# First units loaded as pairs of chunks, W1 in quarters, one PSUM pool and a new order, in a fused RWKV and squared-ReLU kernel

## The chip, the cores and the metric

The kernel runs on one core of a Trainium2 chip. The metric is the device time of one execution in microseconds (us). Three executions took 174.83, 175.56 and 176.46 us, median 175.56. A further execution was profiled; its span, from the first to the last instruction, is 173.7 us.

The core has a matrix engine (PE, with its weight loads shown as PEld), a vector engine (DVE), a scalar engine (ACT), GpSimd (POOL) and a queue engine for transfers (SP). ACT and POOL can issue transfers too. All transfers run on the same 16 DMA engines. Each engine works through its own instructions in order.

## The reference

Two parts follow each other. An attention with a decaying state, over 4 batches, 8 heads, 768 tokens and a head size of 48:

```python
for t in range(S):
    cur = einsum('bhd,bhe->bhde', u * k[t], v[t])
    y[t] = einsum('bhd,bhde->bhe', r[t], state + cur)
    state = w * state + einsum('bhd,bhe->bhde', k[t], v[t])
x = y.transpose(0, 2, 1, 3).reshape(3072, 384)
h = maximum(x @ w_in, 0)          # w_in 384 x 2048
out = (h * h) @ w_out             # w_out 2048 x 384
```

Inputs and output are float32; the products are made in bfloat16.

## The kernel before, in words

The tokens of a batch are cut into 6 chunks of 128, which gives 24 units of one batch and one chunk each. For a unit, r, k and v are tiles of 128 tokens by 8 heads by 48. Inside a chunk the recurrence becomes products: k is scaled by a power of w that falls with the token (`kh`, with the table `Wk`), r by the inverse power (`rh`, with `Wt`), both into the bfloat16 tile `rk`. They are transposed, either on PE (`T`, followed by a copy `Tc` out of PSUM) or by a DMA transpose (`XB`), into `rkT`. `A` makes the 128 by 128 products of k and r for each head, into two banks; `Bm` multiplies them by a triangular mask. `Y` adds the masked products times v (`vb`, v in bfloat16) and, from the second chunk of a batch on, r times the state `S0W`. `U` makes the product of k and v that goes into the state, `S0` (first chunk) or `ts` and `S` (later ones) update it. The term with u is made on the side: `P0` is r times k, `P1` times u, `du` the sum over a head, `dv` that sum times v; `xs` adds it to Y. `X` transposes xs on PE and `xTc` copies it out, or `xX` transposes by DMA.

The FFN takes units in groups: the first two groups have one unit, the other eleven have two. `F1` is a slice of x @ w_in into one PSUM bank (12 products of 128 columns for a single unit, 6 of 256 for a pair; four slices for a single unit, eight for a pair), `re` the ReLU into bfloat16, `sq` the square. `F2` adds a quarter of the second product into one bank for each unit, in the order 0, 1, 2, 3; `os` copies it to SBUF, `out` stores it.

Nothing is scheduled at run time. The string `ORDER` (lines 21 to 106) lists all steps; the loop at lines 499 to 511 takes them one after the other, and each step goes to the engine that stands behind its colon (A, D, G for POOL, P, S for SP). The numbers after the slashes are buffers. So the order of the string, restricted to an engine, is the order of that engine's queue. A step whose input is not ready, or whose buffer is still in use, holds its engine.

What the change touches:
- Units are numbered chunk by chunk: units 0 to 3 are the first chunks of the four batches (`i % B` is the batch, `i // B` the chunk). Each of r, k and v of a unit is one transfer of 128 tokens by 8 heads, in rows of 48 floats, 192 bytes (`ld`, line 319).
- W1 (w_in) comes in slices of 256 columns: seven by `lW` (line 323) into one of four float32 buffers, cast by `cW` (line 259 or 261), one by a casting transfer that POOL issues (`W`, line 332). W2 (w_out) comes in four casting transfers from POOL.
- w goes by DMA to 4 partitions (line 273) and is spread by a shuffle on DVE (line 282); u likewise.
- PSUM has eight banks in three pools: four for the attention, two for F1 (`bH`), two for F2 (`bO`). The early tables `Wk` and `Wt` lie in the two banks of F2 until it starts.
- `Z` (line 480) multiplies the identity into a bank that is not read; the order of before has 139 blocks of 128 columns of it in the first 20 us.

Of the kernel before, what the change touches and what calls it, by code (L numbers as in the profile page):

```python
# [8 lines left out]
FP32 = mybir.dt.float32  # L9
BF16 = mybir.dt.bfloat16  # L10
# [5 lines left out]

GROUPS = [1, 1, 2, 2, 2, 2, 2, 2, 2, 2, 2, 2, 2]
EARLY = 4
POOLS = dict(ldr=7, ldk=7, ldv=7, ws=0, wsa=4, rk=7, P0=5, dv=5, vb=8, rkT=7, bank=4, bankH=2, bankO=2, Bm=6, xs=5, xT1=2, xT2=3, xT4=1, hr=6, hq=30, os=4, ts=2)
ORDER = """  # L20
ld.r.1:S/0 w:A ld.k.1:S/0 u:S Z.48.5:P tab:A ld.k.0:S/1 ld.k.2:S/2 shw:D ld.r.0:S/1 logw:A ld.r.2:S/2 Wt:A/0 P0.1:D/0
shu:D Wk:A/1 lW.0.6:S/0 rh.1:D/0 kh.1:D ld.v.1:S/0 ld.k.3:S/3 T.1:P/0 kh.0:D/1 Z.16.5:P P1.1:G Tc.1:A/0 kh.2:D/2 rh.0:D
ld.v.3:S/1 WtS:A rh.2:D P0.2:G/1 A.1:P/1/2 WkS:A T.0:P/3 lW.0.1:S/1 Z.16.5:P P1.2:D ld.r.3:S/3 Tc.0:A/1 du.1:D/0
P0.0:D/2 cW.0.6:A ld.v.0:S/2 A.0:P/0/3 dv.1:G Bm.1.1:D/0 Z.6.5:P du.2:D/1 T.2:P/2 P1.0:G Bm.1.0:D/1 ld.v.2:S/3 Z.22.5:P
Tc.2:A/2 Bm.0.0:D/2 Bm.0.1:D/3 lW.0.0:S/2 vb.1:A/0 lW.0.5:S/3 kh.3:D/3 Y.1:P/1 cW.0.1:A lW.0.7:S/0 A.2:P/0/2 xs.1:D/0
Z.4.5:P P0.3:G/3 vb.3:A/1 du.0:D/2 lW.0.4:S/1 X.1:P/3 Z.8.5:P rh.3:D wc:S xTc.1:A/0 Bm.2.0:D/4 vb.0:A/2 T.3:P/1
ld.k.4:S/4 dv.0:D Y.0:P/3 Z.13.5:P Tc.3:A/3 vb.2:G/3 Bm.2.1:D/5 P1.3:G xs.0:D/1 A.3:P/0/2 X.0:P/1 cW.0.0:A U.0:P/3
dv.2:G Bm.3.0:D/1 Z.6.7:P xTc.0:A/1 du.3:D/3 lW.0.3:S/2 F1.1.0:P/0 Bm.3.1:D/0 ld.r.4:S/4 F1.0.0:P/1 re.1.0:D/0 W.1.0:G
W.0.2:G cW.0.7:G Y.2:P/0 Y.3:P/1 re.0.0:A/1 ld.k.5:S/5 xs.2:D/2 cW.0.5:A dv.3:D F1.1.3:P/0 cW.0.4:A X.2:P/2 F1.0.3:P/1
re.1.3:D/2 ld.r.5:S/5 xTc.2:A/0 W.1.1:G U.2:P/0 xs.3:D/3 F1.0.2:P/0 re.0.3:A/3 sq.1.3:D2/0 WLcol:A X.3:P/2 F1.1.2:P/1  # L30
re.0.2:D/4 xTc.3:A WLm:G U.3:P/1 F1.2.1:P/0 re.1.2:A/5 W.1.2:G sq.0.3:A0/1 F1.2.5:P/1 re.2.1:D/2 W.1.3:G sq.0.0:A0/2
U.1:P/2 S0.2:D re.2.5:A/3 F1.2.4:P/0 sq.0.2:D2/3 cW.0.3:A S0.0:D F1.2.7:P/1 re.2.4:D/1 sq.1.0:A0/4 F2.0.0:P/1
sq.2.5:D2/5 re.2.7:A/4 S0.3:D F1.0.1:P/0 F1.2.3:P/1 re.0.1:D/0 F2.1.0:P/0 S0.1:D re.2.3:A/3 F1.1.1:P/0 sq.1.2:D2/6
sq.0.1:D2/7 ld.k.7:S/6 F1.2.0:P/1 re.1.1:A/5 F2.0.1:P re.2.0:A/0 sq.1.1:D2/8 F1.2.2:P/0 sq.2.4:A0/9 sq.2.0:D1/10
F2.1.1:P kh.4:D/4 F1.2.6:P/1 ld.v.5:S/4 rh.4:D P0.4:D/4 F2.1.2:P ld.r.7:S/6 re.2.2:D/5 P1.4:G F2.0.2:P re.2.6:D/1
sq.2.2:A0/11 F2.1.3:P ld.v.4:S/5 kh.5:G/5 sq.2.1:A0/12 sq.2.6:D1/13 F2.0.3:P os.1:A/0 du.4:D/4 ld.k.6:S/0 T.4:P/0
sq.2.3:A0/14 rh.5:D F2.2.0:P/0 os.0:A/1 P0.5:D/0 Tc.4:A/4 ld.r.6:S/0 T.5:P/3 P1.5:D F2.2.1:P kh.7:D/6 Tc.5:A/5
ld.v.7:S/6 A.4:P/1/2 du.5:D/0 F2.3.0:P/1 Bm.4.0:D/3 ld.k.9:S/2 A.5:P/0/3 vb.4:A/4 dv.4:G Bm.4.1:D/2 F2.3.1:P vb.5:A/5
ld.r.9:S/2 Bm.5.1:D/4 dv.5:G sq.2.7:A0/15 Y.4:P/1 Bm.5.0:D/5 F2.3.2:P rh.7:G ld.k.8:S/1 xs.4:D/4 U.4:P/2 Y.5:P/3
# [503 lines left out]
```

## Time and profile before

| | us |
|---|---|
| median of three executions | 175.56 |
| lowest, highest | 174.83, 176.46 |
| span of the profiled execution | 173.7 |
| first F1 product starts | 20.48 |
| last product ends | 170.1 |

The page gives, for each engine, the time in which it was busy; `x` counts instructions. A line of a group names the source line, the engine, the operation, the tiles (output, arrow, input), the count, then the busy time, the mean of one instruction in ns, and how long the engine stood idle before them. The groups that matter here:

```profile
L444 PE MATMUL bank<-xT,W 128*128 128x256 bf16 (+1 forms) x624 | 74.5, 264 | 1.3 <-ACT W L259 1.2
L471 PE MATMUL bank<-W,hq 128*128 128x384 bf16 x384 | 73.6, 326 | 0.0
...
L383 DVE TENSOR_TENSOR Bm<-bank,maskJT 128x512 bf16<-128x512 f32 x48 | 31.4, 683 | 3.0 <-PE bank L375 3.0
L345 POOL TENSOR_TENSOR P<-P,ub 128x384 f32<-128x384 f32 x14 | 15.5, 1110 | 30.0 <-DVE P L341 26.8
```

L444 is F1 and L471 is F2. Products overlap in PE's pipeline, so the mean of one is longer than the distance from one to the next; the distances are read from the chain of waits and the timeline. The transfers:

```profile
ldr<-in_r_dram SPq DMA_DIRECT2D x24, 192.0 KB, 3.9
...
wsa<-in_moe_w_in_dram SPq DMA_DIRECT2D x7, 384.0 KB, 5.6
W<-in_moe_w_out_dram POOLq DMA_DIRECT2D x4, 384.0 KB, 7.9
rkT<-rk SPq DMA_TRANSPOSE x14, 3.4
```

The last number is the median time from issue to landing, in us.

### The profile page before, as it was taken

How to read it: one execution, taken by the hardware profiler on the slowest of the kernel's cores; microseconds unless marked ns; L12 is line 12 of the kernel's file. 1: busy time of each engine (PE TensorE's matmuls, PEld its weight loads, DVE VectorE, ACT ScalarE, POOL GpSimd, SP SyncE). 2: the span in 40 equal slices, each digit the busy share in tenths (PEclk: the TensorE clock that was granted, in tenths of full speed). 3: DMA queues.
4: the chain of work that ended last, by engine and by line, in shares of the span. 5: the costliest groups of instructions: out<-in, count | busy, mean ns of one | idle time of the engine just before them, and what ended most of it. 6: DMA issues, size and time to landing. Idle time of an engine off the chain costs nothing.

```text
span 173.7 us, 4402 instructions
## 1 busy us (share of the span) xinstructions
PE 165.4 (95%) x1714; PEld 121.9 (70%) x1714; DVE 140.7 (81%) x278; ACT 109.8 (63%) x203; POOL 69.3 (40%) x84
## 2 busy tenths in 40 slices
PE   4989699999999999999999999999999999999991
PEld 1445498766878787877777787778678677787760
DVE  5989787799899989999989898899998667853520
ACT  2489389557599979786676769659478141173401
POOL 4264743044385694923464950601950301000000
PEclk9999999999999999999999999999999999999999
DMA  5999999999999999989698799989931422110041
GB/s 106 245 249 248 258 213 219 201 192 189 213 188 214 243 171 234 197 191 205 128 217 178 151 205 212 152 191 180 200 94 30 151 94 68 25 45 4 0 171 55
DMA packets 102276, 28.34 MB, mean 163 GB/s; under 512 B 94824, under 2 KB 102256, under 8 KB 102256
## 3 DMA queue, kind: packets, MB, share of 16 engines
q1 hardware_dynamic: 100360, 26.10, 71.4%
q0 software_dynamic: 1744, 1.77, 6.2%
q8 instruction: 13, 0.21, 0.5%
q10 hardware_dynamic: 152, 0.20, 0.3%
q14 instruction: 7, 0.06, 0.1%
HBM read 20.46 MB, written 4.72 MB: 145 GB/s over the span
## 4 chain that ended last, share of the span: by engine, by line
PE 80%; DMA 8%; SPq 6%; ACT 1%; issue 1%; POOL 1%; POOLq 0%
PE bank L471 36%; PE bank L444 33%; DMA wsa<-in_moe_w_in_dram 8%; SPq L319 5%; PE bank L375 3%; PE bank L393 2%; PE bank L391 2%; PE bank L402 2%; PE bank L362 2%; SPq L323 1%; PE bank L428 1%; ACT W L259 1%; ACT hr L452 0%; ACT hq L459 0%; ACT os L259 0%
## 5 line engine op out<-in xcount | busy, mean ns | idle before, releaser
L444 PE MATMUL bank<-xT,W 128*128 128x256 bf16 (+1 forms) x624 | 74.5, 264 | 1.3 <-ACT W L259 1.2
L471 PE MATMUL bank<-W,hq 128*128 128x384 bf16 x384 | 73.6, 326 | 0.0
L452 ACT ACTIVATE hr<-bank 128x512 bf16<-128x512 f32 x71 | 42.0, 597 | 35.9 <-PE bank L444 33.2
L444 PEld LDWEIGHTS <-W 128*128 128x128 bf16 x624 | 55.4, 98 | 11.9 <-ACT W L259 1.4
L471 PEld LDWEIGHTS <-hq 128*128 128x128 bf16 x384 | 35.6, 98 | 17.8
L459 ACT ACTIVATE hq<-hr 128x512 bf16<-128x512 bf16 x57 | 34.7, 629 | 2.5 <-DVE hr L454 2.4
L383 DVE TENSOR_TENSOR Bm<-bank,maskJT 128x512 bf16<-128x512 f32 x48 | 31.4, 683 | 3.0 <-PE bank L375 3.0
L345 POOL TENSOR_TENSOR P<-P,ub 128x384 f32<-128x384 f32 x14 | 15.5, 1110 | 30.0 <-DVE P L341 26.8
L353 POOL TENSOR_TENSOR dv<-ldv,du 128x384 f32<-128x384 f32 x19 | 16.4, 874 | 25.7 <-DVE du L348 21.0
L454 DVE TENSOR_SCALAR hr<-bank 128x512 bf16<-128x512 f32 x25 | 17.1, 689 | 10.4 <-PE bank L444 6.5
L463 DVE TENSOR_TENSOR hq<-hr 128x512 bf16<-128x512 bf16 x35 | 15.0, 457 | 1.9 <-ACT hr L452 1.9
L410 DVE TENSOR_TENSOR xs<-bank,dv 128x384 bf16<-128x384 f32 x24 | 13.2, 553 | 3.5 <-PE bank L393 2.8
L259 ACT COPY os<-bank 128x384 f32<-128x384 f32 x18 | 8.6, 477 | 8.8 <-PE bank L471 8.1
L480 PE MATMUL bank<-identity 128*128 128x512 bf16 (+1 forms) x40 | 11.6, 427 | 2.3 <-POOL identity masks.py:199 2.3
L348 DVE TENSOR_REDUCE du<-P 128x8 f32<-128x384 f32 x24 | 12.9, 543 | 0.0
L341 POOL TENSOR_TENSOR P<-ldr,ldk 128x384 f32<-128x384 f32 x11 | 11.3, 1026 | 3.9 <-DMA ldr<-in_r_dram 3.9
L259 ACT COPY rkT<-bank 128x1024 bf16<-128x1024 bf16 x10 | 10.1, 1015 | 2.9 <-PE bank L362 2.2
L423 POOL TENSOR_TENSOR S0W<-ts,WLm 128x384 bf16<-128x384 f32 x7 | 7.4, 1061 | 10.0 <-PE bank L471 6.7
L393 PE MATMUL bank<-vb,Bm 128*128 128x48 bf16 x192 | 10.8, 183 | 0.3 <-ACT vb L259 0.3
L393 PEld LDWEIGHTS <-Bm 128*128 128x128 bf16 x192 | 9.5, 96 | 1.3 <-issue 0.4
L259 ACT CAST vb<-ldv 128x384 bf16<-128x384 f32 x19 | 9.6, 511 | 0.2 <-DMA ldv<-in_v_dram 0.2
L259 ACT COPY xT<-bank 128x384 bf16<-128x384 bf16 x14 | 6.5, 477 | 5.0 <-PE bank L428 5.0
(61 smaller groups left out, 161.7 us busy)
## 6 DMA issues: line engine op xcount, KB each, us to landing
ldr<-in_r_dram SPq DMA_DIRECT2D x24, 192.0 KB, 3.9
ldk<-in_k_dram SPq DMA_DIRECT2D x24, 192.0 KB, 3.8
ldv<-in_v_dram SPq DMA_DIRECT2D x24, 192.0 KB, 4.0
out_dram<-os SPq DMA_DIRECT2D x23, 192.0 KB, 2.2
wsa<-in_moe_w_in_dram SPq DMA_DIRECT2D x7, 384.0 KB, 5.6
W<-in_moe_w_out_dram POOLq DMA_DIRECT2D x4, 384.0 KB, 7.9
rkT<-rk SPq DMA_TRANSPOSE x14, 3.4
W<-in_moe_w_in_dram POOLq DMA_DIRECT2D x1, 192.0 KB, 8.2
```

The costliest lines, as they stand in the source:

```text
L259: e.copy(o, a)
L345: e.tensor_mul(t, t, ub)
L353: e.tensor_mul(dvb[slot[f"dv{i}"]], loaded("v", i), t)
L383: e.tensor_mul(Bmb[slot[f"Bm{i}{h}"]], heads(bank(f"bA{i}{h}"), 128), mask_b)
L393: e.matmul(y[:, hc, D * h : D * (h + 1)], m[h][:, hc, :], vb[:, 2 * hc + h, :], start=(c == 0), stop=True, skip_group_check=True,)
L410: e.tensor_add(xsb[slot[f"xs{i}"]].rearrange("p (a b) -> p a b", a=HP), heads(bank(f"bY{i}"), 2 * D), dvb[slot[f"dv{i}"]].rearrange("p (a ...
L444: e.matmul(hp[:, fi, :], W1[f // 2][:, c, 128 * (f % 2) : 128 * (f % 2 + 1)], xt[:, c, :], start=(c == 0), stop=(c == CCH - 1), skip_group ...
L452: e.activation(hr, hp, AF.Relu)
L454: e.tensor_scalar_max(hr, hp, 0.0)
L459: e.activation(hq, hr, AF.Square)
L463: e.tensor_mul(hq, hr, hr)
L471: e.matmul(bank(f"bO{i}", "bO")[:, 0:d_model], hqb[slot[f"hq{g},{f // m}"]][:, at : at + L], W2[q][:, f % 4, :], start=(f == 0), stop=(f = ...
```

## The change

Units are listed in a table. Units 0 and 1 are the first two chunks of batch 0, units 2 and 3 those of batch 1; batches 2 and 3 follow, and from unit 8 on the order is chunk by chunk. The first four units are loaded in pairs: partition p of a pair holds tokens 2p and 2p + 1 of the 256, so that a row is 96 floats, 384 bytes, and chunk c of the pair lies in partitions 64c to 64c + 63. A tile that `loaded` gives for such a unit holds the even or the odd tokens of both chunks. `Ap`, `Bp`, and the new branches of `Y` and `U` therefore work on halves of 64 rows, with masks `maskP`; `Y` adds the u term by two products with the identity, so `xs` of these units is a plain copy. For them the transposes of k and r are separate steps (`TK`, `TR`, copies `KC`, `RC`), and the tables have three columns (even, odd, and the plain one for later units).

W1 comes in four transfers of 512 columns into three buffers, cast in halves by ACT, DVE or POOL; none comes by a casting transfer. w goes to all 128 partitions by one transfer, and the shuffle goes. The eight PSUM banks are one pool. The four quarters of F2 may come in any order. The order is new throughout. Counted in the two strings: loads 72 become 60 and 6 of pairs; `XB` 14 become 18, `T` 10 become 2 (and 2 `TK`, 2 `TR`), `X` 14 become 8, `xX` 10 become 16; on POOL `kh` 5 become 15, `rh` 6 become 13, `P0` 11 become 16, `vb` 3 become 11, `cW` 1 become 4; on ACT `re` 71 become 64, `sq` 57 become 44; on DVE `re` 25 become 32, `sq` 39 become 52; fill 139 blocks of columns become 81.

```diff
+UNITS = [(0, 0), (0, 1), (1, 0), (1, 1), (2, 0), (3, 0), (2, 1), (3, 1), (0, 2), (1, 2), (2, 2), (3, 2), (0, 3), (1,
+    3), (2, 3), (3, 3), (0, 4), (1, 4), (2, 4), (3, 4), (0, 5), (1, 5), (2, 5), (3, 5)]
+PAIRED = 4
-POOLS = dict(ldr=7, ldk=7, ldv=7, ws=0, wsa=4, rk=7, P0=5, dv=5, vb=8, rkT=7, bank=4, bankH=2, bankO=2, Bm=6, xs=5, xT1=2, xT2=3, xT4=1, hr=6, hq=30, os=4, ts=2)
+POOLS = dict(ldr=8, ldk=8, ldv=8, ws=3, rk=7, P=5, dv=5, vb=8, rkT=7, bank=8, Bm=8, xs=5, xT1=2, xT2=3, hr=6, hq=28,
+    os=4, ts=2)
 ORDER = """
-ld.r.1:S/0 w:A ld.k.1:S/0 u:S Z.48.5:P tab:A ld.k.0:S/1 ld.k.2:S/2 shw:D ld.r.0:S/1 logw:A ld.r.2:S/2 Wt:A/0 P0.1:D/0
...
+w:A lp.k.0:S/0 tab:A u:S lp.r.0:S/0 lp.r.1:S/1 lp.k.1:S/1 lp.v.0:S/0 logw:A Wk.1:A kh.1:D/0 shu:D Wk.0:A lp.v.1:S/1
+Wt.0:A rh.0:D/1 kh.0:G/1 Wt.1:A rh.1:G/0 P0.0:D/0 wc.1:A lW.1:S/0 P0.1:D/1 Z.56:P/0 TK.0:P/0 KC.0:A/0 rh.2:D/2 Wt.2:A
+P1.0:G lW.0:S/1 P1.1:D du.1:D/0 Z.5:P/1 TR.0:P/1 RC.0:A/1 lW.2:S/2 kh.3:G/3 kh.2:D/2 ld.k.4:S/4 Z.20:P/2 Ap.0.0:P/2/3
+rh.3:D/3 du.0:D/1 vb.0:A/0 wc.0:A P0.3:G/2 TK.1:P/4 ld.r.4:S/4 Ap.0.1:P/5/6 Bp.0.0.1:D/0 dv.1:G TR.1:P/7 vb.2:A/1
+ld.v.4:S/4 vb.3:D/2 dv.0:G Bp.0.1.0:D/1 vb.1:A/3 WLcol:A P1.3:G U.2:P/0 U.1:P/1 Bp.0.1.1:D/2 KC.1:A/2 U.0:P/3 U.3:P/5
+WLm:G RC.1:A/3 Bp.0.0.0:D/3 Y.0:P/6 xs.0:A/0 S0.0:D ts.1:D/0 cW.2:G Y.1:P/4 cW.3:G du.3:D/2 Wk.2:A S0.2:D X.0:P/7
+P0.2:G/3 Ap.1.1:P/2/6 xTc.0:A/0 xs.1:D/1 Ap.1.0:P/3/1 Bp.1.1.0:D/4 cW.1:A W.0:G X.1:P/0 F1.0.1:P/7 P1.2:D xTc.1:A/1
+F1.1.1:P/4 W.1:G cW.0:A lW.3:S/0 ts.3:D/1 re.0.1:A/0 Bp.1.1.1:D/5 F1.0.0:P/0 ld.r.5:S/5 du.2:D/3 cW.4:A cW.5:G dv.2:D
+F1.1.0:P/5 Bp.1.0.0:D/6 re.0.0:A/1 dv.3:G F1.1.2:P/7 Bp.1.0.1:D/7 re.1.0:A/2 ld.k.5:S/5 F1.0.2:P/0 kh.4:G/4 re.1.2:D/3
+sq.1.0:A/0 Y.2:P/5 xs.2:A/2 re.1.1:D/4 rh.4:G/4 re.0.2:D/5 sq.0.2:D/1 Y.3:P/7 P0.4:G/4 T.4:P/5 xs.3:A/3 X.2:P/4
+X.3:P/0 xTc.2:A/0 F2.1.0:P/7 ld.r.6:S/6 xTc.3:D/0 vb.4:G/4 Tc.4:A/4 sq.1.2:D/2 P1.4:G F1.2.4:P/4 F1.2.2:P/0 re.2.4:D/2
...
         def w(e):
-            e.dma_start(out=quarter_rows(wrow), in_=row4(w))
+            e.dma_start(out=wb.rearrange("p a b -> p (a b)"), in_=spread(w, 128))
...
+        def lp(e, x, q):
+            b, c = UNITS[2 * q]
+            e.dma_start(
+                out=ld[x][slot[f"p{x}{q}"]].rearrange("p (h m) -> p h m", h=H),
+                in_=src[x].rearrange("b h (c p a) d -> b c p h (a d)", p=128, a=2)[b, c // 2],
+            )
+
+        def lW(e, q):
+            e.dma_start(out=wsb[slot[f"ws{q}"]], in_=w_in_t[:, :, 512 * q : 512 * (q + 1)])
...
+        def Ap(e, q, a):
+            kT, rT = (
+                rkTb[slot[f"{n}{q}"]].rearrange("p x y -> p (x y)").rearrange("p (h c t) -> p h c t", h=HP, c=2)
+                for n in ("kT", "rT")
+            )
+            for hc in range(HP):
+                for c in range(2):
+                    for h in range(2):
+                        p0 = 64 * h
+                        e.matmul(
+                            heads(bank(f"bA{q}{a}{h}"), 128)[64 * c : 64 * c + 64, hc, :],
+                            kT[p0 : p0 + D, hc, c, 64 * a : 64 * a + 64],
+                            rT[p0 : p0 + D, hc, c, :],
+                            start=True, stop=True, skip_group_check=True,
+                        )
...
         def Y(e, i):
...
+            if i < PAIRED:
+                q, s = i // 2, i % 2
+                rows = slice(64 * s, 64 * s + 64)
+                for a in range(2):
+                    e.matmul(
+                        y[64 * a : 64 * a + 64], identity[rows, rows],
+                        dv_of(2 * q + a)[rows].rearrange("p (a e) d -> p a (e d)", e=2),
+                        start=True, stop=False, skip_group_check=True,
+                    )
...
+                for hc in range(HP):
+                    for h in range(2):
+                        for a in range(2):
+                            e.matmul(
+                                y[:, hc, D * h : D * (h + 1)],
+                                Bmb[slot[f"Bm{q}{a}{h}"]][rows, hc, :],
+                                vbb[slot[f"vb{2 * q + a}"]][rows, 2 * hc + h, :],
+                                start=False, stop=True, skip_group_check=True,
+                            )
+                return
...
         def F2(e, i, q):
...
-                    start=(f == 0), stop=(f == FCH - 1), skip_group_check=True,
+                    start=(seen[i] == 1 and f % 4 == 0), stop=(seen[i] == 4 and f % 4 == 3), skip_group_check=True,
```

## The prediction

> **What bounds the kernel now.** First the page: busy time and the forty slices.
>
> ```profile
> PE 165.4 (95%) x1714; PEld 121.9 (70%) x1714; DVE 140.7 (81%) x278; ACT 109.8 (63%) x203; POOL 69.3 (40%) x84
> ...
> PE   4989699999999999999999999999999999999991
> ...
> DMA  5999999999999999989698799989931422110041
> ```
>
> From the fifth slice on PE has no gap; DVE is near 95% in the middle and the DMA engines are full up to slice 28 of 40. So the time is: when dense work on PE begins, plus the PE work left, plus a tail. The chain of waits says what sets the beginning and the end:
>
> ```profile
> 13.93 5.59 DMA wsa<-in_moe_w_in_dram
> 19.54 0.88 ACT W L259
> ...
> 20.45 8.05 DMA wsa<-in_moe_w_in_dram
> ...
> 163.57 6.51 PE bank L471 x40
> 170.11 0.48 ACT os L259
> ```
>
> The slices of W1 arrive late: one lands at 13.93 + 5.59 = 19.52, ACT casts it, and then the first product of the FFN runs (timeline, both rows PE):
>
> ```profile
> 2.35 5.30 PE L480 MATMUL bank<-identity 128*128 128x512 bf16 x12 [2.35 <-POOL identity masks.py:199]
> ...
> 20.48 1.51 PE L444 MATMUL bank<-xT,W 128*128 128x128 bf16 x24 [1.23 <-ACT W L259]
> ```
>
> Check of this reading, with spacings from the chain and the timeline: F1 0.655 us per step of 256 columns (0.67 for a single unit), F2 0.65, T 0.45, A 0.38 with the 0.1 that the next product loses, Y 0.375, U and X 0.17. From the end of the first F1 step (21.15) remain 88 F1 at 0.655, 7 at 0.67, 96 F2, 6 T, 20 A, 22 Y, 19 U, 12 X: 148.6 us. 21.15 + 148.6 = 169.7; the last product ended at 170.1. PE lost 0.4 us in 149. The tail to 173.7 is 3.6.
>
> **The profiled execution** spans 173.7 us, the median of the runs is 175.56; I add the 1.86 between them to every span below.
>
> **Transfer prices.** Stretches of the window view (last columns: DMA share, GB/s):
>
> ```profile
> 2.00:4.00 2.00, 1.66 (x4) 0.58 (x5) 1.35 (x9) 1.28 (x1) 0.73 (x3) 1.00 1.03 199
> 4.00:6.00 2.00, 2.00 (x6) 0.76 (x5) 1.84 (x6) 1.32 (x3) 0.12 (x1) 1.00 1.08 213
> ...
> 16.00:18.00 2.00, 1.96 (x25) 1.06 (x25) 2.00 (x5) 1.59 (x3) 1.71 (x3) 1.00 0.95 281
> 18.00:20.00 2.00, 1.16 (x17) 0.69 (x16) 2.00 (x4) 0.46 (x1) 2.00 (x4) 1.00 0.87 273
> ...
> 80.00:100.00 20.00, 20.00 (x220) 14.58 (x219) 18.43 (x36) 14.14 (x29) 11.24 (x12) 1.00 0.85 173
> ```
>
> Rows of 192 bytes alone run at 206 GB/s, W1's rows of 1 KB at 277. A fixed part and a part per byte through both points gives 245 GB/s at 384 bytes and 289 at 2 KB (estimates from these rows; bounds 206 and 277). The twelve early loads (2.36 MB) then take 9.6 us where they took 11.45: 1.8 gained, 0 at the lower bound, 2.9 at the upper.
> [...]
>
> **The beginning, step by step.** w goes to 128 partitions: 0.197 MB, about 0.96 at 206 GB/s, so it lands at 4.95 instead of 3.99, but the shuffle (0.58) goes. logw to 5.5, then Wk.1, Wk.0, Wt.0, Wt.1 at 0.58 each to 7.8. DVE in the new order: kh.1 to 6.6, shu, rh.0, P0.0, P0.1, rh.2, P1.1, du.1, kh.2, rh.3, du.0 (0.55 to 0.6 each) to 12.25, one Bp (0.68) to 12.95, then vb.3. That waits for lp.v.1: 2.0 (first bytes) + 0.7 (w) + 9.6 + 1.8 = 14.1, where 1.8 is the lag between bytes and landing (by the same sum the old slice is moved at 17.7 and landed at 19.52). Three more Bp end at 16.6. Y.0, 18 products, I put at 0.9 (0.54 if its 384-column pair overlaps, 1.2 by T's 0.056 a product), Ap, 16 products on quarter tiles, at 0.7 (0.33 as A, 1.0 as two T), U at 0.34. ACT's queue holds WLcol behind the small transfer wc.0; the old one took 6.6 us in SP's queue, w's took 2.6 on ACT's; at 2.6 it hides behind vb.2 and vb.1, at 6.6 KC.1, RC.1, xs.0 and, on POOL, WLm and the casts move by some 2 us. I take the former, as it is the same queue. RC.1 to 17.5, xs.0 to 18.05, xTc.0 to 19.1, X.1 to 20.2 (Y.1 now waits for S0.0, which is done at 17.2, before Y.0 leaves PE): the first F1 starts at 20.2, hardly earlier than 20.48.
> W1's quarters (0.786 MB, 2.7 each) land at 16.8, 19.5, 22.2; the third, cast by ACT and POOL, lets F1.1.2 start at 23.3. Then F1.0.2, Y.2, Y.3, T.4, X.2, X.3 to 27.25. F2.1.0 also needs W.0, which POOL issues behind its longer row of products: about 19.1, and the landing row says
>
> ```profile
> DMA to landing us min/median/max: 7.1/8.2/9.1
> ```
>
> so 27.3 (26.2 to 28.7). F2.1.0 ends at 27.95.
>
> **PE work left then:** 88 F1, 2 single F1, 95 F2, 1 T, 20 A, 20 Y, 16 U, 4 X = 139.7. In the old kernel 142.2 were left at that moment. The whole gain is that 4 Ts and 6 Xs are now DMA transposes (1.8 + 1.0); the earlier start of the FFN gives nothing by these sums. W.2 is queued on POOL behind kh.4, rh.4, P0.4, vb.4, P1.4 (4.6 us): issued about 28, landed 36.2, wanted at 35.8; I take 0.4 (0 to 2.3). PE runs in order, so all that follows F2.1.2 waits with it. Sum: 27.95 + 139.7 + 0.4 (PE's old losses) + 0.4 + 3.6 = **172.0, time 173.9** (1% less).
>
> **Elsewhere.** ACT gives up some 25 us (13 squares, 7 Relus, 8 vb, 6 copies of transposed r and k, 8 xT), at no effect: it idles 64 now. DVE's sum stays within 3 us (13 squares and 7 Relus more, 17 kh and rh, 5 P0, 3 xs less). POOL takes 10 kh, 7 rh, 5 P0, 8 vb, 3 casts more: +30 us to 99; hidden under PE after 40 us, not before (T.4 waits on rh.4 with 0.5 to spare). SP's queue loses 12 loads (0.6 each) and gains 6 pairs, 4 DMA transposes of rk (1.5) and 6 of xs (1.2): even in sum, but from unit 6 instead of 9. Free F2 order, the shared PSUM pool and the larger Bm pool cost nothing by themselves: they move waits.
>
> **Rivals.**
> 1. *DMA becomes the bound (slower).* Summing the window view, the old kernel had moved 8.5 MB at 40 us, 16.7 at 80, 20.2 at 100. Up to XB.14 the new order moves 19.7 MB (6 pairs, W1, W2 at 1.57, 43 loads, 10 transposes of rk, 4 of xs, 5 outputs). At the old pace, less the 2.4 gained at the start, that is 94.9, plus lag 1.8; A.14 is wanted at 93.6: 3.1 late, and 5.0 if the two more rk and two more xs transposes cost their issue time. At XB.10 the old kernel had moved its 13.5 MB by 63.9 and wanted A.10 at 69: 5 us in hand. Time 177.0 to 178.9. It decides from a lateness of 1.7 (slower at all), 3.5 (by 1%). Against: the old pace was not the limit (173 GB/s at share 0.85 above; 240 in the first 30 us).
> 2. *PE at half speed.* The twelve fill products took 0.43 each up to 7.5 us, later ones 0.21, with a granted clock of 1.00 throughout. The new order has 81 instead of 139 blocks of 128 columns of fill. If PE drops back between 13 and 20 us, the first F1 steps cost double: 0.5 to 2.5 more, time 174.4 to 176.4. Against: its products fill most of that stretch.
> 3. *POOL holds DVE up.* Squares on DVE (shortest, median, longest):
>
> ```profile
> L463 DVE TENSOR_TENSOR hq<-hr x3: 412/414/1006, 59.2 to 76.8; 128x512 bf16<-128x512 bf16 x3
> ```
>
> Some 600 ns is lost now and then; over squares, kh, rh, P and S the means exceed the shortest by about 4.5 us in all, with POOL at 69. At 99 it is 2 us more on DVE, which has 5.4 us of idle time between 40 and 120: time 173.9 to 175.9.
> [...]
> 4. *The larger packets gain nothing:* everything up to the third quarter is 1.8 later; time 175.7.
>
> **Numbers.** This kernel's runs scatter by about 1%, so 1% (1.76 us) is what a measurement can tell. Forecast case 0.54: its own range by the bounds above (W.0 and W.2, wc.0, Y and Ap) 172.2 to 175.5, faster 0.41, same 0.13. Rival 1: 0.24 (same 0.06, slower 0.18). Rival 2: 0.07 (same 0.05, slower 0.02). Rival 3: 0.08 (faster 0.02, same 0.04, slower 0.02). Rival 4: 0.07 (faster 0.01, same 0.04, slower 0.02). Together faster 0.44, same 0.32, slower 0.24. Range 171.8 to 178.2.
>
> **What would show it.** First F1 near 20 and F2.1.0 near 27.5 with W.0's landing just before it; quarters landing near 17, 19.5, 22; PE without gaps after 37 and DMA transposes issued before their A is next; F2 products to the end. Wrong if PE waits for rkT again and again between 45 and 110 (rival 1), if F1's products are 0.21 apart (2), if DVE's long squares multiply (3), or if the early loads land at the old pace (4).

## The result, and the profile after

The changed kernel took 195.19 us (median of four executions, 192.19 to 196.1), the kernel before 175.23 beside it. The ratio, 1.1014 with a 95% interval of 1.0907 to 1.112, is of the fast executions alone, 192.19 and 194.65 us of the changed kernel, since the other two count as slow. The forecast was 173.9 us (171.8 to 178.2). The profiled execution spans 190.5 us, 16.8 more than the 173.7 of before.

The page of the changed kernel, busy times and slices:

```profile
PE 169.9 (89%) x1733; PEld 123.4 (65%) x1733; DVE 156.5 (82%) x274; ACT 88.9 (47%) x163; POOL 108.4 (57%) x134
...
PE   4948997998989899997699599999998899999992
...
PEclk9996579799999999999999999999999999999999
```

PE, without a gap from the fifth slice on before, now has gaps over the whole run, and the granted clock falls to half in the first part. DVE is busy 15.8 us longer and POOL 39.1; ACT is 20.9 us lighter. The chain of waits, by engine, was 80% PE before; now it runs as much through DVE:

```profile
DVE 39%; PE 36%; DMA 12%; issue 6%; POOL 3%; ACT 2%; SPq 1%; DVEq 0%; POOLq 0%; ACTq 0%
```

**Where the 16.8 us are.** The window view, cut at 36 us, gives PE's busy time after it, which is the work then left, and so PE's idle time: 134.1 and 3.6 us before, 141.4 and 13.1 after. So 7.3 us were lost in the first part, and 9.5 us later. The worst of the later windows (columns: window, length, busy time of PE, PEld, DVE, ACT, POOL with counts, granted clock, DMA share, GB/s):

```profile
80.00:100.00 20.00, 17.43 (x169) 13.61 (x168) 16.09 (x31) 9.26 (x18) 13.14 (x14) 1.00 0.83 171
100.00:120.00 20.00, 17.23 (x179) 12.45 (x177) 19.18 (x31) 7.86 (x16) 15.96 (x16) 1.00 0.84 169
```

The second of them in the kernel before:

```profile
100.00:120.00 20.00, 20.00 (x207) 15.53 (x206) 18.27 (x36) 15.29 (x31) 5.62 (x7) 1.00 1.05 186
```

PE loses 2.6 and 2.8 us of 20; beside it POOL is at 13 to 16 of 20 (11.2 and 5.6 before), and from 100 on DVE has no room.

**What DVE does there.** Two groups of DVE with the mean of one instruction in ns (before: squares 457, Bm 683):

```profile
L509 DVE TENSOR_TENSOR hq<-hr 128x512 bf16<-128x512 bf16 x52 | 29.6, 585 | 3.5 <-ACT hr L500 3.2
L406 DVE TENSOR_TENSOR Bm<-bank,maskJT 128x512 bf16<-128x512 f32 x40 | 25.8, 678 | 1.8 <-PE bank L398 1.8
```

The square, both of whose operands lie in SBUF, is slower; Bm, one of whose operands is in PSUM, is not. The timelines of DVE and POOL laid over each other tell why. Counting the rows of a single instruction in the changed kernel that lie wholly outside POOL's instructions, and those with at least 80% of their time under them (mean us, count):

| DVE instruction | operands | alone | under POOL |
|---|---|---|---|
| square | SBUF, SBUF | 0.42 (13) | 0.84 (15) |
| rh | SBUF, SBUF | 0.54 (1) | 0.84 (7) |
| P1 | SBUF, SBUF | 0.55 (1) | 0.94 (5) |
| du | SBUF | 0.54 (9) | 0.54 (12) |
| Bm | PSUM, SBUF | 0.68 (6) | 0.68 (9) |
| xs | PSUM, SBUF | 0.55 (4) | 0.54 (7) |

The longest case, from the timelines of DVE (first) and POOL of the changed kernel:

```profile
25.56 3.53 DVE L342 TENSOR_TENSOR dv<-ldv,du 128x384 bf16<-128x384 f32 x1
...
25.75 1.02 POOL L324 TENSOR_TENSOR rk<-ldk,Wk 128x384 bf16<-128x384 f32 x1
26.71 1.01 POOL L327 TENSOR_TENSOR rk<-ldr,Wt 128x384 bf16<-128x384 f32 x1
27.67 0.99 POOL L330 TENSOR_TENSOR P<-ldr,ldk 128x384 f32<-128x384 f32 x1
28.61 0.84 POOL L263 CAST vb<-ldv 128x384 bf16<-128x384 f32 x1
```

dv.2, 0.55 us by itself, started while POOL's dv.3 ran, stood through kh.4, rh.4 and P0.4, which followed each other without a gap, and ended 0.48 us after vb.4, a cast, had begun. In the table it is DVE's products of two SBUF operands that lose (square 0.42 to 0.84 us), while du (0.54), Bm (0.68) and xs (0.55 and 0.54) keep their time. By what means POOL holds them up, no trace here shows.

I call *blocked time* what the products of two SBUF operands on DVE took above 0.42 us (square) and 0.55 us (others; 0.08 less for each further one in a row of several, as three kh in a row took 1.48 us in the kernel before), summed from the timeline. In the kernel before it is 4.9 us (0.1 ahead of 36 us, 4.8 after it), in the changed kernel 24.7 us (7.2 and 17.5). This rise of 19.8 us, less some 4 us of other work that DVE gave up, is the 15.8 us by which it is busy longer. From 36 us on, 19 of DVE's 87 products of two SBUF operands met one of POOL's in the kernel before, and 49 of 91 in the changed one.

### The profile page after: what moved, and what is told of

Same layout as the page of the kernel before. It is cut to its first block, busy times and chain, and to the rows that moved or that the text cites. A ratio compares the mean times of both kernels' runs of the same rounds, so it can differ in the third digit from the quotient of the medians.

```text
span 190.5 us, 4445 instructions
## 1 busy us (share of the span) xinstructions
PE 169.9 (89%) x1733; PEld 123.4 (65%) x1733; DVE 156.5 (82%) x274; ACT 88.9 (47%) x163; POOL 108.4 (57%) x134
## 4 chain that ended last, share of the span: by engine, by line
DVE 39%; PE 36%; DMA 12%; issue 6%; POOL 3%; ACT 2%; SPq 1%; DVEq 0%; POOLq 0%; ACTq 0%
PE bank L492 17%; PE bank L518 13%; DVE Bm L406 10%; DVE hq L509 6%; DMA ldr<-in_r_dram 4%; DMA wcol<-in_w_dram 4%; DVE rk L327 3%; DVE xs L462 3%; DVE hr L502 3%; DVE du L337 3%; DVE P L330 2%; DVE rk L324 2%; DMA ldv<-in_v_dram 2%; DMA rkT<-rk 2%; DVE P L334 2%
## 5 line engine op out<-in xcount | busy, mean ns | idle before, releaser
L500 ACT ACTIVATE hr<-bank 128x512 bf16<-128x512 f32 x64 | 36.4, 596 | 41.1 <-PE bank L492 31.3
L518 PEld LDWEIGHTS <-hq 128*128 128x128 bf16 x384 | 35.6, 98 | 22.2 <-DVE hq L509 2.1
L507 ACT ACTIVATE hq<-hr 128x512 bf16<-128x512 bf16 x44 | 26.7, 631 | 18.3 <-DVE hr L502 17.9
L509 DVE TENSOR_TENSOR hq<-hr 128x512 bf16<-128x512 bf16 x52 | 29.6, 585 | 3.5 <-ACT hr L500 3.2
L406 DVE TENSOR_TENSOR Bm<-bank,maskJT 128x512 bf16<-128x512 f32 x40 | 25.8, 678 | 1.8 <-PE bank L398 1.8
L342 POOL TENSOR_TENSOR dv<-ldv,du 128x384 f32<-128x384 f32 (+1 forms) x19 | 17.8, 944 | 13.6 <-DVE du L337 9.5
L330 POOL TENSOR_TENSOR P<-ldr,ldk 128x384 f32<-128x384 f32 x16 | 17.6, 1100 | 8.4 <-DMA ldr<-in_r_dram 8.4
L324 POOL TENSOR_TENSOR rk<-ldk,Wk 128x384 bf16<-128x384 f32 x15 | 18.0, 1200 | 1.3 <-ACT Wk L282 0.7
L327 POOL TENSOR_TENSOR rk<-ldr,Wt 128x384 bf16<-128x384 f32 x13 | 14.6, 1130 | 6.3 <-DMA ldr<-in_r_dram 6.3
L261 ACT COPY os<-bank 128x384 f32<-128x384 f32 x16 | 7.6, 477 | 17.5 <-PE bank L518 12.4
L462 DVE TENSOR_TENSOR xs<-bank,dv 128x384 bf16<-128x384 f32 x20 | 10.7, 545 | 1.5 <-POOL dv L342 0.9
L398 PE MATMUL bank<-rkT 48*128 48x128 bf16 x160 | 7.3, 217 | 4.6 <-DMA rkT<-rk 2.3
L327 DVE TENSOR_TENSOR rk<-ldr,Wt 128x384 bf16<-128x384 f32 x11 | 10.3, 937 | 0.1
```

What stands on the lines that cost most here:

```text
L324: e.tensor_mul(rk[slot[f"rk{i}"]][:, 1, :, 0:D], loaded("k", i), Wk[:, i % 2 if i < PAIRED else 0])
L327: e.tensor_mul(rk[slot[f"rk{i}"]][:, 0, :, 0:D], loaded("r", i), Wt[:, i % 2 if i < PAIRED else 0])
L330: e.tensor_mul(P0b[slot[f"P{i}"]], loaded("r", i), loaded("k", i))
L406: e.tensor_mul(Bmb[slot[f"Bm{i}{h}"]], heads(bank(f"bA{i}{h}"), 128), mask_b)
L500: e.activation(hr, hp, AF.Relu)
L507: e.activation(hq, hr, AF.Square)
```

## The experiments

Each is an edit of one of the two kernels; the steps are those of the order string, the letter behind the colon is the engine. The theories are numbered anew in each group of expectations. "Left" is PE's busy time after 36 us, "idle" its idle time after it, "blocked" DVE's blocked time ahead of 36 us and after; these come from the one profiled execution.

| run | ratio to before (95%) | span | left | idle | blocked |
|---|---|---|---|---|---|
| before | 1 | 173.7 | 134.1 | 3.6 | 0.1, 4.8 |
| after | 1.101 (1.091 to 1.112) | 190.5 | 141.4 | 13.1 | 7.2, 17.5 |
| a_pool_back | 1.107 (1.101 to 1.114) | 193.4 | 140.2 | 17.2 | 6.5, 16.4 |
| b_pool_load (of before) | 1.030 (1.023 to 1.037) | 180.6 | 137.9 | 6.7 | 0.3, 18.1 |
| a_wc_early | 1.093 (1.085 to 1.101) | 192.5 | 142.0 | 14.5 | 8.4, 20.9 |
| a_sq_act | 1.077 (1.071 to 1.084) | 189.4 | 142.2 | 11.2 | 7.8, 18.1 |
| c_old_split | 1.088 (1.079 to 1.097) | 192.3 | 140.4 | 15.9 | 5.2, 12.8 |
| c_fill | 1.097 (1.091 to 1.104) | 192.9 | 143.2 | 13.7 | 7.6, 18.4 |
| c_split_fill | 1.109 (1.099 to 1.118) | 193.2 | 139.7 | 17.5 | 4.8, 12.6 |
| b_w_all (of before) | 1.006 (1.002 to 1.010) | 175.6 | 136.0 | 3.6 | 0.3, 4.8 |
| d_new_start | 1.132 (1.125 to 1.140) | 197.5 | 145.7 | 15.8 | 7.0, 6.6 |
| d_old_start | 1.175 (1.170 to 1.181) | 206.1 | 141.8 | 28.3 | 0, 16.1 |
| d_ld_early | 1.136 (1.128 to 1.144) | 199.4 | 145.5 | 17.9 | 7.4, 18.1 |
| d_ld_split | 1.118 (1.106 to 1.130) | 194.1 | 140.1 | 18.0 | 5.9, 12.0 |
| e_level | 1.072 (1.067 to 1.077) | 186.9 | 139.6 | 11.3 | 8.7, 11.0 |
| e_old_level (of before) | 1.005 (1.002 to 1.008) | 175.5 | 135.3 | 4.2 | 0.1, 13.0 |
| e_pool_cut | 1.055 (1.049 to 1.061) | 184.4 | 140.5 | 7.9 | 9.2, 5.4 |
| f_psum_pool (of before) | 0.996 (0.993 to 1.000) | 173.8 | 134.1 | 3.7 | 0, 4.8 |
| f_w1_quarters (of before) | 1.028 (1.020 to 1.035) | 178.5 | 139.2 | 3.3 | 0.3, 5.5 |
| f_cut_fill | 1.058 (1.049 to 1.067) | 185.1 | 138.7 | 10.4 | 9.4, 4.6 |

### POOL's load: put back in the new kernel, put into the old one

a_pool_back gives kh, rh, P0 and vb of units 4 to 23 the engines of before, in the new order:

```diff
-kh.4:G/4
+kh.4:D/4
-vb.4:G/4
+vb.4:A/4
```

> The new kernel with the engine of kh, rh, P0 and vb of units 4 to 23 as in the old one (42 steps leave or change POOL; kh and rh go to DVE, vb to ACT; the order is the new one). Theory 1 (POOL holds DVE up: DVE's instructions with two inputs in SBUF exceed their shortest by some 25 us in the new kernel, by 5 in the old): DVE gets about 9 us more of its own work and still the time falls by 6 to 12 us, and the mean of DVE's squares falls from 585 ns toward 460. Theory 2 (DVE simply has too much to do): the time stays or rises by up to 9 us. Theory 3 (the start and the late transposes by DMA are the loss): within 2 us of the new kernel.

b_pool_load does the reverse to the kernel before, in its own order.

> The old kernel with the engine of kh, rh, P0 and vb of units 4 to 23 as in the new one, nothing else changed: POOL gets about 24 steps more, DVE about 13 fewer. Theory 1 (POOL holds DVE up): slower by 4 to 10 us, with DVE's squares at a mean above 520 ns instead of 457. Theory 2 (the sum of DVE's work): no slower, 174 to 176 us.

In the kernel before, the load alone made 3.0% (2.3 to 3.7). Its squares (457 ns before) and kh (634):

```profile
L463 DVE TENSOR_TENSOR hq<-hr 128x512 bf16<-128x512 bf16 x35 | 17.5, 528 | 3.4 <-ACT hr L452 3.4
L335 DVE TENSOR_TENSOR rk<-ldk,Wkhat 128x384 bf16<-128x384 f32 x7 | 7.6, 1092 | 0.0
```

DVE was busy 4 us longer though it had 20 products fewer, and 13 us of blocked time came in. So the blocking is real and is not tied to the new order. But taking the load back in the new order won nothing: POOL fell from 108.4 to 82.6 us, and DVE's busy time rose to 163.8, with blocked time still at 16.4 after 36 us. Of the first part a_pool_back shows one thing. With kh.4, rh.4, P0.4 and vb.4 off POOL, dv.2 takes 0.67 us in place of 3.53:

```profile
25.42 0.67 DVE L341 TENSOR_TENSOR dv<-ldv,du 128x384 bf16<-128x384 f32 x1
```

The first F2 product then starts at 30.92 in place of 32.99, but the work left at 36 us falls by 1.2 us only.

### The late small transfer, and squares to ACT

a_wc_early issues the two transfers `wc` at the head of ACT's queue; a_sq_act moves every second square of DVE, from group 2 on, to ACT (23 of them).

```diff
-wc.0:A
+wc.1:A wc.0:A
...
-sq.2.2:D/6
+sq.2.2:A/6
```

> The new kernel with the two small transfers of w by head (wc) issued at the very start on ACT's queue, before the logarithm, so that the step WLcol on ACT does not stand waiting from 14.6 to 18.6 us. If that wait holds the start (it stands in the chain of waits), the first F1 comes 2 to 4 us earlier than 23.4 and the time falls by 2 to 4 us; if the next thing behind it (POOL, or the casts and W2's transfers) is as late, by less than 1.

> The new kernel with every second square of groups 2 to 12 that DVE makes moved to ACT, which idles 100 us: 23 steps, 0.41 us each on DVE at their shortest, 0.63 on ACT. Theory 1 (POOL holds DVE up, and the squares are its commonest victim): the time falls by 5 to 9 us. If the late transposes by DMA or the order hold PE instead: less than 2.

The transfer was on the chain (it landed 6.67 us after its issue), but with it out of the way the intervals overlap: in the profiled execution the first F1 started 0.64 us earlier and the first F2 0.41 us later. DVE's blocked time ahead of 36 us was 8.4 us in place of 7.2, so its products are the likely next link; that is read, not tested. The squares moved gave 2.4% in the ratio, about 4.3 us, a little short of theory 1's 5 to 9; those left on DVE were still slow (mean 662 ns).

### The whole split among the engines, and the half clock

c_old_split gives the squares and ReLUs of groups 2 to 12 their old engines too. c_fill puts products of the identity into PE's gaps; c_split_fill does both.

```diff
-Z.20:P/2 Ap.0.0:P/2/3
+Z.60:P/2 Ap.0.0:P/2/3
...
-Y.2:P/5
+Z.24:P/5 Y.2:P/5
```

> The changed kernel in its own order, but every elementwise product, cast, ReLU and square of units 4 to 23 (groups 2 to 12) stands on the engine that it had in the kernel before: kh, rh, P0 and vb as in the run a_pool_back, and besides 78 of the re and sq steps. DVE then has 39 squares and 25 ReLUs in place of 52 and 32, ACT 57 and 71 in place of 44 and 64. From 36 us to the end PE stood idle for 13.1 us in the changed kernel (154.5 us less 141.4 us busy), 3.6 us in the kernel before. Theory 1 (the load on DVE and POOL and their blocking one another is what stops PE in the dense stretch): PE's idle time after 36 us falls to 3.5 to 7 us, the span to 181 to 185 us, and the mean of the squares left on DVE to under 500 ns. Theory 2 (the new order of PE's work, its fewer turns on the banks and its transposes through DMA stop PE, whichever engine does the products): idle time after 36 us stays at 11 us or more and the span at 188 us or more.

> The changed kernel with products of the identity put in PE's gaps of the first part (104 more of 128 columns, at five places ahead of Ap, TK.1, U.2, Y.0 and Y.2); nothing that is read changes. In the changed kernel the granted clock was half for 10.2 us from 15.7 us on and for 3.4 us from 32.8 us on. Theory 1 (the half clock delays the first part, and the clock falls because PE had stood idle): the clock is full up to 40 us, the first F2 comes 3 to 6 us earlier than 33.0 us, and the run is 3 to 6 us shorter. Theory 2 (PE waits for DVE, ACT and transfers in that part, so that a faster PE only waits longer): the clock is full, the first F2 comes less than 1.5 us earlier and the time stays within 1.5 us. Theory 3 (it is not idle time that takes the clock down): the clock is half again for about as long.

> Both edits at once: the split of the kernel before among the engines, and the identity products in the gaps. If the late start (7.3 us of PE's work more left at 36 us than in the kernel before) and the idle time after 36 us (9.5 us more) are made by these two causes, the span comes to 176 to 180 us; if the order itself is the cause, it stays above 186 us.

c_fill cut the half clock ahead of 36 us from 13.6 to 3.4 us, and the ratio stayed within its interval; but its clock fell to half for 6.8 us from 108.7 us on, so f_cut_fill below is the cleaner test. The old split in the new order took blocked time away (17.5 to 12.8 us) and left 15.9 us of idle time, as theory 2 of c_old_split had it. c_split_fill, with both edits, stayed at 193.2 us, above the 186 from which its expectation blamed the order itself. So theory 1 of c_old_split fell in its simple form: the old split, which serves the old order, doesn't serve the new one. In c_old_split 34 of 92 products of two SBUF operands on DVE still met one of POOL's after 36 us, so the new order brings them together more often even with the old split. Which of its steps come late there wasn't tried.

### w to all partitions, alone

b_w_all makes this part of the change in the kernel before.

```diff
-            e.dma_start(out=quarter_rows(wrow), in_=row4(w))
+            e.dma_start(
+                out=wb.rearrange("p a b -> p (a b)"),
+                in_=bass.AP(tensor=w.tensor, offset=w.offset, ap=[[0, 128], [1, H * D]]),
+            )
```

> The kernel before with one part of the change alone: w is sent to all 128 partitions by its own transfer, and the shuffle (0.58 us on DVE) with the memset ahead of it is gone. In the kernel before wb was ready at 4.60 us; in the changed kernel the wide transfer landed at about 5.45 us. Theory 1 (the wide transfer is the slower way under the first rows' load): wb is ready 0.3 to 1 us later than before, and the time is 0 to 1 us longer. Theory 2 (as the prediction had it, the transfer lands by 4.95 us, and less work on DVE makes up for it): the time stays within 0.4 us or is shorter.

It costs 0.6% (0.2 to 1.0) by itself, which is theory 1's size, but not by its way. In the profiled execution w landed at 4.50, no later than the 4.60 at which the shuffle of before was done. The first rows came later instead: r's first transfer landed at 5.22 in place of 3.48 and k's at 5.99 in place of 4.64. DVE's first product, which began at 4.74 before, waited for k, and the first F1 started 2.1 us later than its 20.48:

```profile
6.09 0.56 DVE L339 TENSOR_TENSOR P<-ldr,ldk 128x384 f32<-128x384 f32 x1 [2.71 <-DMA ldk<-in_k_dram]
...
22.61 1.51 PE L442 MATMUL bank<-xT,W 128*128 128x128 bf16 x24 [1.41 <-ACT W L257]
```

### Orders joined, and loads moved forward

d_new_start follows the new order up to unit 7 and the old one from unit 8 on; d_old_start is the reverse. Both needed buffers and banks given out anew and a few steps put ahead of others where the two halves meet. In d_old_start the quarters of F2 come in the new order, for which that kernel's flag for the first product of a sum isn't made, so that parts of the sums are dropped; the instructions are the same. d_ld_early moves loads forward in SP's queue; d_ld_split adds the edits of c_split_fill.

```diff
-xTc.2:A/0 F2.1.0:P/7 ld.r.6:S/6
+ld.r.6:S/6 xTc.2:A/0 F2.1.0:P/7
```

> The changed kernel up to unit 7 (groups 0 to 4), followed by the kernel before's order and engines for units 8 to 23 (groups 5 to 12), which are the same work with the same steps in both kernels; buffers and banks are given out anew for the joined order (6 output buffers and 3 for ts in place of 4 and 2). Theory 3 (after the splits of the runs a_pool_back and c_old_split left the dense stretch as it was, the cause is the new order itself: products are asked of DVE, POOL and the load queue too shortly before PE takes them): PE's idle time after 80 us falls from 10.8 us to about the 3.6 us of the kernel before and the span from 190.5 to 182 to 185 us, the rest being the late start. Theory 1 (late start and blocking carry through the whole run, whatever the order): the idle time after 80 us stays at 8 us or more and the span at 188 us or more.

> The other way round: the kernel before up to unit 7, with the changed kernel's order and engines for units 8 to 23. Nothing of the change's loading, packets, 64-row products or clock is left in it. Theory 3 (the order): the first 80 us are as in the kernel before and PE then stands idle for 5 to 8 us more, so that the span is 179 to 182 us. Theory 1 (the new order only suffers from its start): the span stays within 2 us of the kernel before's 173.7 us.

> The changed kernel with the loads of units 6 to 23 placed earlier in SP's queue, by up to 6 us of PE's work each, ahead of the transposes and output stores that they stand behind; their buffers have been free by then for 17 us or more. POOL waited for ldr in the changed kernel for 8.4 and 6.3 us in all (3.9 us in the kernel before), and the chain of waits passes through a load at 83, at 127 and at 136 us. Theory 3a (of the order, it is the loads standing behind waiting transposes that cost most): these waits fall below 4 us and the span falls by 3 to 7 us, to 184 to 187 us. Theory 3b (the short leads between DVE or ACT and PE cost it, the loads are only one of several steps as late): the waits fall, but the span changes by less than 2 us.

> Early loads, the kernel before's split among the engines and the identity products in the gaps of the first part, all together in the changed kernel's order. If the loads and the engines' load bound the dense stretch in turn, each hiding the other, the span falls to 178 to 183 us here, though the split with the identity products alone left it at 193.2 us; if the order of PE's own work is what it waits on, it stays at 187 us or more.

None was faster than the changed kernel: three were slower by 3 to 7%, and d_ld_split's interval overlaps its own. d_old_start and d_ld_early missed both of their theories. d_new_start met its theory 1 (idle time of 8 us or more after 80 us, span of 188 or more) and d_ld_split its second case (187 or more), but these had no upper end. The joined orders tell the theories apart no further, since the seam and the new buffers cost something that the runs don't separate. One number of d_new_start bears on the argument: its blocked time after 36 us is down to 6.6 us and PE is idle for 15.8 us, so little blocked time alone doesn't keep PE busy. d_ld_early can be read: POOL's waits for ldr are gone from the list, and PE waits for something else (columns: what waits, for what, us in all, times, longest):

```profile
PE bank L491 <- DMA xT<-xs: 7.6, 3, 3.8
```

The loads now stand ahead of the DMA transposes of xs in SP's queue, and F1 waits for those, at most 1.2 us in all before the edit. In this queue, which is worked in order, moving the loads forward moved the transposes back.

### DVE levelled, and POOL's work taken away

e_level keeps the new order and moves 122 elementwise steps so that no stretch asks DVE for much more than PE's time; e_old_level does the like to the kernel before. e_pool_cut keeps order and engines and shortens POOL's products of units 8 to 23: they are computed for the first of 8 heads only.

```diff
+    def cut(e, i):
+        return 1 if e is nc.gpsimd and i >= 8 else H
...
-            e.tensor_mul(P0b[slot[f"P{i}"]], loaded("r", i), loaded("k", i))
+            n = cut(e, i)
+            e.tensor_mul(P0b[slot[f"P{i}"]][:, 0:n], loaded("r", i)[:, 0:n], loaded("k", i)[:, 0:n])
```

> The changed kernel's steps in the changed kernel's order; 122 of its elementwise steps stand on another engine, chosen so that DVE is never asked for much more than PE's own time in any stretch: 29 fewer squares on DVE (23 in place of 52; ACT 73 in place of 44), more of kh, rh, P0, P1, S and dv on POOL. Counted with the shortest durations, DVE was asked for 14.1 us and POOL for 12.3 us of work in the stretch of the order in which PE has 12 us (units 10 to 13) and ACT for 3.4 us; here it is 9.9, 15.7 and 6.4 us. In the traces a product of two SBUF operands on DVE takes twice its time while POOL runs one (square 0.42 to 0.84 us, product 0.55 to about 1.0 us), one that reads PSUM does not. Theory 4 (DVE's products doubled by POOL's, in clumps where DVE had no room, make the idle time of PE in the dense stretch, and neither the order of PE's work nor POOL's own load does): PE's idle time after 36 us falls from 13.1 to 4 to 7 us and the span from 190.5 to 181 to 185 us. Theory 3 (PE's order): idle stays at 11 us or more. Theory 5 (the more POOL works, the worse): slower than 192 us.

> The kernel before with its steps and order as they are and 113 elementwise steps on other engines by the same count: DVE has 28 squares in place of 39, and POOL 13 kh, 16 rh, 17 P0 and 18 P1 in place of 5, 6, 11 and 14. PE was busy all of 36 to 160 us in the kernel before, so there is little to win: theory 4 expects 172.5 to 175 us of span; theory 5 (the more POOL works, the worse, as the run b_pool_load with 20 more POOL products went to 180.6 us) 178 us or more.

> The changed kernel, order and engines unchanged, but the products that stand on POOL for units 8 to 23 (kh, rh, P0, P1, S, and dv from unit 12 on) are computed for the first of 8 heads only (S: the first of 4 pairs); the rest of these tiles keeps older values. POOL then hardly blocks DVE after about 70 us, and its results come about 0.8 us earlier each. Theory 4 (blocking): the mean of DVE's squares falls from 585 to under 480 ns, PE's idle time after 80 us from 10.8 to 4 to 6 us, the span to 184 to 187 us. Theory 3 (PE's order or the loads, whatever POOL does): idle after 80 us stays at 9 us or more and the span at 189 us or more.

e_pool_cut decides the dense stretch. Its chain by engine, and its windows beside those shown above:

```profile
PE 64%; DVE 14%; DMA 11%; issue 4%; SPq 2%; ACT 2%; POOL 1%; POOLq 0%; DVEq 0%; ACTq 0%
```

```profile
80.00:100.00 20.00, 17.87 (x175) 14.02 (x174) 15.71 (x32) 9.87 (x19) 7.12 (x18) 1.00 0.93 179
100.00:120.00 20.00, 20.00 (x217) 14.34 (x215) 18.08 (x36) 9.21 (x18) 6.89 (x16) 1.00 0.97 189
```

With the same order, the same instructions on DVE and the same start, DVE's blocked time after 36 us falls from 17.5 to 5.4 us, PE's idle time from 13.1 to 7.9, and the ratio by 4.7 points, some 8 us (6.1 us between the two profiled spans). Its idle time after 80 us, 7.0 us, is still above the 4 to 6 that theory 4 expected. From 100 to 120 PE has no gap left. The edit shortens POOL's products as well as the blocking, so the two aren't separated; the load on POOL as a whole is shown to cost this. From 80 to 100 PE still loses 2.1 us: there the chain passes through a load queue step, an `XB` of 3.9 us and its A, as it does with loads and `XB` between 120 and 140. That rest, some 4 us of idle time above the 3.6 of before, was read from the chain, not tried with success. With the 6.4 us more of work left at 36 us it makes up the 10.7 us by which e_pool_cut's span still exceeds the 173.7 of before.

e_level won 3 points of the 10 and missed its range: DVE has room, but POOL is full from 100 to 120 (19.54 of 20 us), and `XB`, whose input POOL makes, is late (PE waits 4.0 us for rkT). Its expectation speaks of clumps in DVE's work. Counted in the traces, over 108 us of PE's work from 36 us on and with DVE's instructions at their undisturbed prices, the kernel before asks DVE for some 105 us, the changed one for 106 and e_level for 90; the fullest stretch of 12 us holds 13 to 14 us in the first two, depending on where the cuts lie. So neither clumps nor DVE's own work are the difference between the two kernels. DVE had little room for blocked time in either, and the old one had 4.8 us of it where the new one has 17.5. In the kernel before, 37 us more on POOL with DVE levelled (e_old_level) cost 0.5% (0.2 to 0.8), its span of 175.5 just outside theory 4's 172.5 to 175; b_pool_load, with 28 us more on POOL and DVE as it was, cost 3.0%. This fits that blocked time costs where DVE has no slack for it.

### One PSUM pool, W1 in quarters, and the first part once more

```diff
-    first = {"b": 0, "bH": POOLS["bank"], "bO": POOLS["bank"] + POOLS["bankH"]}
+    first = {"b": 0, "bH": 0, "bO": 0}
...
-lW.0.6:S/0
+lW.3:S/0
```

> The kernel before with one part of the change alone: its 8 PSUM banks are one pool (given to each product in the order in which they came free) in place of 4, 2 and 2 for three kinds of products. Order, engines and buffers are as they were. Theory 4 (blocking and load make the loss): within 1 us of the kernel before. Theory 3b (PE waits for banks that another kind of product still holds): 2 to 6 us longer, with PE idle in 36 to 160 us, where it had no idle time.

> The kernel before with one part of the change alone: W1 comes in four quarters of 768 KB in place of seven eighths of 384 KB and one eighth by POOL's casting transfer; POOL casts that eighth instead (0.88 us). In the kernel before the first F1 began at 20.5 us and its weights' halves of a quarter landed one by one; a quarter took 7.4 us to land in the changed kernel, an eighth 5.6 us in the kernel before. Theory A (larger pieces arrive later, and the first F1 waits for its quarter): the first F1 begins 0.5 to 2 us later and the time is 0.5 to 2 us longer. Theory B (as the prediction had it, the quarters land in time): the time stays within 0.5 us.

> The run e_pool_cut (POOL's products of units 8 to 23 computed for one head of 8; the output is not the full computation) with the first part helped besides: the identity products of c_fill in PE's gaps and the two small transfers of w first on ACT's queue, as in a_wc_early. In e_pool_cut 140.5 us of PE's work were left at 36 us, 134.1 us in the kernel before. Theory A (half clock and the late transfer, 6 and 4 us by themselves, hold the first part up, one hiding the other): 134 to 137 us are left at 36 us and the span falls from 184.4 to 179 to 182 us. Theory B (the first rows, which land at 7.8 us in place of 4.7 us, and DVE's and POOL's first products on them set the first part): the span changes by less than 1.5 us.

One pool of banks costs nothing (0.993 to 1.000). f_w1_quarters gives no price for the quarters: my edit put the second quarter's load ahead of the cast of W1's last eighth, which uses the same buffer, so that this eighth was cast from the wrong quarter and F1 waited 2.8 us for the cast by POOL; the 2.75% contain that wait. Ahead of it, though, the first F1 came at 22.96 in place of 20.48. A load of r that stands behind a quarter in SP's queue landed at 18.15 (14.94 before), and DVE stood 2.2 us for it. So a larger piece did delay the start in the order of before, through the rows behind it rather than, as theory A had it, through its own landing. f_cut_fill has the full clock throughout:

```profile
PEclk9999999999999999999999999999999999999999
```

Its work left at 36 us fell by 1.8 us, its idle time after that rose from 7.9 to 10.4 us, and its time did not fall (1.058, with an interval of 1.049 to 1.067, against 1.055). So the half clock and the late small transfer together make at most 1.8 of the 6.4 us by which the first part of e_pool_cut is late. The span changed by 0.7 us, as theory B had it; but the cause that theory B names, the late first rows, was not tried by itself.

## Why the prediction was wrong

- **The failed step** is "hidden under PE after 40 us", said of POOL's additional load, together with rival 3's "At 99 it is 2 us more on DVE". POOL came to 108 us and the blocked time rose by 19.8 us, not 2. I scaled the excess of before (4.5 us) a little with POOL's busy time. But the excess hangs on how often, and for how long, a product of DVE meets one of POOL, and the order of before kept the two apart: after 36 us the meetings rose from 19 to 49, POOL's time in products of two operands only from 55 to 75 us. And DVE's 5.4 us of idle time from 40 to 120, against which I set it, is less than what came. b_pool_load shows the effect without the new order. e_pool_cut shows what POOL's load costs in the new one, the blocking and the length of POOL's own products together: 4.7 of the 10 points. Rival 3 had the right cause, at a chance of 0.08 and a tenth of its size.
- **What stays open:** the late first part and some 4 us of idle time, 10.7 us of span together in e_pool_cut. c_split_fill and d_new_start show that the old split, or little blocked time, doesn't by itself close PE's gaps in a new order.
- **DVE's products in the first part, "0.55 to 0.6 each"**, were the same mistake. The timeline shows rh.2 at 1.35 and P1.1 at 1.35 under POOL's P1.0, kh.3 and P0.3, then dv.2 at 3.53: 7.2 us of blocked time ahead of 36 us, against 0.1. The first part is 7.3 us late. That these agree isn't proof. a_pool_back took the row over dv.2 away, and the first F2 came 2.1 us earlier; no run took POOL's products of the first four units away, so the rest stays argued.
- **First F1 at 20.2, F2.1.0 at 27.3:** they came at 23.39 and 32.99 (timeline of PE), so 5.7 of the 18.5 us between the forecast span of 172.0 and 190.5 lie ahead of F2.1.0. It wasn't held by W.0, as the sum had it (that landed at 30.28), but by Y.2 and Y.3 ahead of it on PE, which waited for dv.2 and the Bp behind it on DVE.
- **wc.0 "at 2.6":** it landed 6.67 us after its issue, the other bound. a_wc_early shows that it wasn't worth the 2 us that I gave it: the first F1 came 0.64 us earlier without it.
- **Rival 2 (half speed)** came, for 13.6 us in place of a few, and cost nothing in the time that f_cut_fill or c_fill could show. In the changed kernel PE did the F1 products from 23.39 to 28.7, at half speed until 25.7, and then stood waiting for dv.2 all the same.
- **Transfer prices:** too low, so they aren't what made the kernel late: lp.v.1 landed at 13.55 (forecast 14.1), the first three quarters at 15.89, 18.36 and 20.39 (16.8, 19.5 and 22.2). From 6 to 10 us only the pairs' rows of 384 bytes moved, from 14 to 18 us only the quarters' of 2 KB:

```profile
6.00:8.00 2.00, 2.00 (x6) 0.76 (x5) 1.13 (x4) 1.97 (x5) 1.19 (x4) 1.00 1.06 273
8.00:10.00 2.00, 2.00 (x21) 1.28 (x20) 2.00 (x3) 0.88 (x2) 1.60 (x2) 1.00 1.05 276
...
14.00:16.00 2.00, 1.65 (x32) 1.29 (x32) 2.00 (x4) 0.59 (x2) 1.04 (x2) 0.87 1.05 381
16.00:18.00 2.00, 1.25 (x25) 1.09 (x26) 2.00 (x4) 0.00 (x0) 1.84 (x2) 0.50 1.07 382
```

The pairs, at 273 and 276 GB/s, ran at my upper bound of 277, where the sum took 245, and the quarters, at 381 and 382, above my 289. Rival 4, by which the larger packets gain nothing, would have had the pairs at the 206 of 192-byte rows; these windows speak against it here. Yet the first pieces came later: k's pair landed at 6.65 and r's at 7.85, where single transfers of r and k had landed at 3.48 and 4.64. DVE's first product, which needs k's pair and the table Wk.1 (ready at 6.65 too), began at 6.75 in place of 4.74. So the larger first pieces came faster by the byte here (199 and 213 GB/s in the windows of before) and later by the piece; with the wide w alone, in b_w_all, r's and k's single transfers landed at 5.22 and 5.99.
- **Right:** the PSUM pool as free of cost (f_psum_pool). Half right: w's wide transfer was put at 4.95, and logw, which waits for it, began at 5.49. What the sum had too small is its weight on the rows behind it (0.7 us): in b_w_all, in the order of before, it moved the first F1 by 2.1 us, and the time by 0.6%. Rival 1 (DMA as the bound) came in part: after 36 us POOL waited 14.7 us for ldr (8.4 and 6.3, in two groups), PE 2.3 us for rkT, but d_ld_early, which took the waits for ldr away, was slower.

## What to carry to other kernels

Before moving a product of two SBUF operands from DVE to POOL, count what DVE still does with two SBUF operands at that moment. Here those that met POOL took some 1.5 to 2 times their time (0.84 to 0.94 us in place of 0.42 to 0.55), and one that met a row of three of POOL's products without a gap took 3.53 us and ended after the row. How often they meet is set by the order as well as by the load: 19 times after 36 us in the old order, 34 times with the same split in the new one (c_old_split). Read an engine's slack from the dense stretch, not from its share of the span (DVE's 81% were 74.6 us of the 80 from 40 to 120). The squares given to ACT, which was free, were the simplest move that gained here (a_sq_act). In a kernel with hand-ordered queues the order and the split among engines are one choice: here POOL's new load in the old order cost 3% (b_pool_load), and the old split in the new order won little (c_old_split).

## What was not expected of the hardware

POOL is slowed too: its products of two SBUF operands take 1.00 us alone (rh, P0 and P1 of the changed kernel) and 1.15 to 1.21 us with one of DVE's beside them (these and kh, which never ran alone). The granted clock stayed at half from 15.5 to 25.7 us though PE was busy for 1.9 to 2.0 of every 2 us from 18 us on. It was half for 10.2 us there and for 3.4 us from 32.6 us on. What sets these lengths, and why the clock wasn't back to full soon after 18 us, isn't shown.
